# One table of steps for attention's engines: the two-unit order, doubled runs of value products and a block-diagonal left tile

## The chip, the cores and the metric

The kernel runs on one core of a Trainium2 chip. The metric is the device time of one execution in microseconds. Of the kernel before there are three runs: median 634.83 us, from 632.91 to 635.03. One further execution was recorded by the profiler; it spans 631.5 us, and all rows below are of that one. A difference of 0.5% is about what a measurement of this kernel can tell.

## The reference

Three layers follow one another: attention over 4 batches of 8 heads (576 rows of 64 values each) that keeps only scores near each row's maximum, a soft mixture of 8 experts with 4 slots each, and a gated feed-forward layer. All is float32.

```python
scores = scale * np.matmul(q, k.transpose(0, 1, 3, 2))
thresh = np.max(scores, axis=-1, keepdims=True) - tau
scores = np.where(scores >= thresh, scores, -1000000000.0)
attn = np.exp(scores - np.max(scores, axis=-1, keepdims=True))
attn = attn / (np.sum(attn, axis=-1, keepdims=True) + 1e-09)
x = np.matmul(attn, v)                     # heads side by side: 2304 x 512
...
logits = x @ phi                           # 32 slots
d = softmax(logits, axis=0);  slot_input = d.T @ x
h = np.maximum(slot_input[e] @ w1[e], 0.0);  slot_out[e] = h @ w2[e]
x = softmax(logits, axis=1) @ slot_out
...
h = x @ w_in
return (h * (1.0 / (1.0 + np.exp(-1.702 * h)))) @ w_out
```

## The kernel before

**Units and tiles.** A unit is one pair of heads of one batch: 16 units (NU), 4 to a batch. Of a head's 576 rows 512 make four tiles of 128, and the last 64 are the left rows (R). A unit has nine score tiles (TPU): four pairs, one tile for each head, and a ninth that holds the left rows of both heads. `scores` (line 392) makes a pair at once: the two heads lie on the two halves of the partitions, so their products run in the two half arrays of TensorE (form 64\*128 in the profile, rows by columns), two halves of 288 columns each, two passes for each product. The left tile's products use quarter arrays (64\*64). A score tile takes two of the eight PSUM banks, and there are two such tiles (`ps_s`).

**One tile's way.** `row_max` (416) on VectorE copies the scores to SBUF (p) and finds the row's extreme; GpSimd adds the threshold (th); `exps` (435) on ScalarE; `mask` (442) on VectorE multiplies and sums (l); `trans` (497) transposes the weights by 128\*128 products with ident on TensorE, into one of two banks (`ps_t`), and its `after` copies them on ScalarE (pt, ptr). When four or five tiles (a half) are done, `inverse`, `widen` and `across` turn the sums' reciprocals into a row (l, lw, l_row), and `attn_v` (556) multiplies with the values: v_left in the full array, then for each of four blocks kc the two heads' products in the two column halves (form 128\*64). VectorE scales the result into xt (`o_ps`, one bank).

**Other steps.** `prep_main` and `prep_rest` transpose the next unit's q and k; they, `x_rows` and the logits take the same two banks `ps_t` or parts of the bank `r_ps`. At the end of a batch the logits of 32 slots are made, their running maximum and slot sums updated. Pieces of w_in are decoded beside it, on ScalarE, VectorE and GpSimd (`decoding`, 153), one piece in five steps (PACE). Loads are issued on SP's queue.

**What sets the order.** A loop over tiles i (line 800) calls each step at a fixed distance: row_max(i-1), exps(i-1), trans(i-4), scores(i) at even tiles, mask(i-2), and, counted from a unit's start, the reciprocals at 6 and 11, the row's transposes at 9 and 14, blocks of value products at 10, 12, 14 and 16. What a step leaves behind (`after`) is called in the next round. The class InOrder (line 124) records each operation (so all of attention's operations have line 134 in the profile) and keeps it in the program's order on its engine; SP's loads are not kept so.

**Behind attention.** When attention's pools close, weights of the experts are loaded into rings a, b, c and so on, each placed in a freed pool (`swap`, line 118; the DMAs of lines 913 and 101). The expert products (L968, L1003) and the feed-forward part (L1176 to L1204) follow. The change does not touch them.

Of the kernel before, what the change touches and what calls it, by code (L numbers as in the profile page):

```python
# [8 lines left out]
F32 = mybir.dt.float32  # L9
# [10 lines left out]
def kernel(  # L20
# [37 lines left out]
    PACE = 5  # L58
# [94 lines left out]
    def decoding(pool, key, n, finish):  # L153
# [7 lines left out]
        if key[0] == "in":  # L161
            po.tensor_scalar(
                out=rest, in0=lo, scalar1=2.0 ** -52, scalar2=1.0, op0=ALU.mult, op1=ALU.mult
            )
# [72 lines left out]
    def attention():  # L237
# [28 lines left out]
        ve.memset(v_left, 0.0)  # L266
        xt = tx.tile([P, HP, C * P], F32, name="xt")
# [8 lines left out]
        def load_rests(b):  # L276
            n = {}
            for nm, src in (("q", q), ("k", k)):
                r = ldq.tile([R, H, D], F32, tag=nm + "r", name=f"{nm}r")
                nc.sync.dma_start(out=r, in_=src[b, :, C * P:S, :].rearrange("h p d -> p h d"))  # L280
                n[nm] = r
            rest[b] = n
# [32 lines left out]
        def turned(u, nm):  # L315


            if (u, nm) not in qk:
                n = S if nm == "q" else S + R
# [3 lines left out]
        def prep_rest(u, bank):  # L323
            b, hp = divmod(u, HP)
            t = bank([P, 2, R], "rem_t")
            for j, nm in enumerate("qk"):
                te.transpose(
                    t[:, j, :],
                    rest[b][nm][:, 2 * hp:2 * hp + 2, :].rearrange("p h d -> p (h d)"),
                    ident[0:R, 0:R],  # L330
                )
# [9 lines left out]
        def prep_main(u, nm, bank):  # L341
# [7 lines left out]
            def after():  # L349
                out, src = turned(u, nm)[:, R:S], t.rearrange("p c t -> p (c t)")  # L350
                if nm == "q":
                    ac.activation(out=out, in_=src, func=AF.Copy, scale=neg if u else 1.0)
                else:
                    ac.copy(out=out, in_=src)
# [37 lines left out]
        def scores(i):  # L392
# [3 lines left out]
            qx, kx = qk[u, "q"], qk[u, "k"]  # L396
            heads = [slice(h * D, (h + 1) * D) for h in range(2)]
            if t < 2 * C:
                both = [ps_s.tile([P, 2, 512], F32, tag="s", name="s_ps") for _ in range(2)]
                s_ps[i], s_ps[i + 1] = both  # L400
                c0 = R + t // 2 * P
# [14 lines left out]
        def row_max(i):  # L416

            u, t = divmod(i, TPU)
            if t % 2 == 0:
# [6 lines left out]
                scalar1=1.0 if u else neg, scalar2=None, op0=ALU.mult, op1=ALU.min,  # L426
# [3 lines left out]
            if t % 2 or t == 2 * C:  # L430
                mns.pop((u, t // 2))
            thr[i] = sm.tile([P, 1], F32, tag="th", name="th")
            po.tensor_tensor(out=thr[i], in0=mn, in1=tau_p, op=ALU.add)

        def exps(i):
            e = sx.tile([P, S], F32, tag="e", name="e_sb")
            ac.activation(
                out=e, in_=weights(i), func=AF.Exp, bias=m_neg.pop(i), scale=-1.0
# [3 lines left out]
        def mask(i):  # L442
# [3 lines left out]
            if t in (0, C):  # L446
# [6 lines left out]
            if t in (C - 1, 2 * C):  # L453
# [865 lines left out]
```

## Time and profile before

| | |
|---|---|
| median of 3 runs | 634.83 us (632.91 to 635.03) |
| the profiled execution's span | 631.5 us |
| TensorE (PE) busy | 610.9 us, 97% |
| VectorE (DVE) | 400.4 us, 63% |
| ScalarE (ACT) | 371.5 us, 59% |
| GpSimd (POOL) | 151.0 us, 24% |
| first scores | 10.7 us |
| end of attention (slot sums scaled) | 354.5 us |
| first products of the slot outputs with w_in (wq) | 395.3 us |

Records of matmuls overlap, since the engine is pipelined; so in the timeline one reads from one row's start to the next row's start. A product of two passes shows as two records: a run of four score products has x8. The span has three stages: attention to 354.5 us, the experts to 395 us, the feed-forward layer to the end. The waits are told by the instruction that waits and by what released it.

### The profile page before, as it was taken

Reading aid. Unit: us, or ns where it says so; the run is one execution under the profiler, and the core shown is the slowest. Engines: PE = TensorE matmul, PEld = TensorE weight load, DVE = VectorE, ACT = ScalarE, POOL = GpSimd, SP = SyncE. Lnnn points to the kernel's source line nnn. Section 1 sums busy time; section 2 is a strip of 40 time slices with the busy share of each in tenths; the row PEclk is TensorE's granted clock in tenths of the full one; section 3 lists DMA queues with packets and bytes.
Section 4 is the critical chain, followed back from the end, with each engine's and each line's share of the span. In section 5 each row is a group of like instructions: output and inputs, shape, how many; then the busy total and the mean of one; then the engine's idle time right before and its main releaser. Section 6 shows DMA issues by size and latency. Waiting matters only on the chain.

```text
span 631.5 us, 10661 instructions
## 1 busy us (share of the span) xinstructions
PE 610.9 (97%) x3778; PEld 417.3 (66%) x3778; DVE 400.4 (63%) x1015; ACT 371.5 (59%) x776; POOL 151.0 (24%) x309
## 2 busy tenths in 40 slices
PE   7999999999999999999998999899999999999996
PEld 5666665666666666665665642577877788888884
DVE  2987877787886877778773242999995221332422
ACT  2878877777786787877773010757576353333340
POOL 0445453354443354543341010000300000000000
PEclk9999999999999999999999989999999999999999
DMA  7984222232232132224517999333520000020203
GB/s 186 314 283 112 69 58 63 55 90 65 56 81 53 52 86 70 70 51 149 171 57 269 326 390 377 101 104 101 167 101 0 1 0 1 16 85 1 102 1 100
DMA packets 67110, 69.97 MB, mean 111 GB/s; under 512 B 42736, under 2 KB 46832, under 8 KB 67056
## 3 DMA queue, kind: packets, MB, share of 16 engines
q1 hardware_dynamic: 67056, 69.28, 34.7%
q8 instruction: 30, 0.49, 0.3%
q14 instruction: 24, 0.20, 0.1%
HBM read 64.55 MB, written 4.72 MB: 110 GB/s over the span
## 4 chain that ended last, share of the span: by engine, by line
PE 85%; DVE 5%; DMA 5%; ACT 2%; issue 1%; SPq 1%; DVEq 0%
PE s_ps L134 15%; PE o_ps L134 14%; PE pt_ps L134 11%; PE y_ps L1202 10%; PE y_ps L1203 10%; PE y_ps L1204 10%; PE r_ps L134 5%; DMA w_b<-in_moe_w_dram 3%; PE h_ps L1176 2%; DMA raw<-in_moe_w_out_dram 2%; PE acc L968 2%; PE q_t L134 2%; PE k_t L134 2%; DVE p L134 1%; PE x_ps L134 1%
## 5 line engine op out<-in xcount | busy, mean ns | idle before, releaser
L134 DVE TENSOR_SCALAR_CACHE_REDUCE p<-s_ps 128x576 f32<-128x576 f32 x135 | 101.7, 754 | 55.1 <-PE s_ps L134 49.0
L134 ACT ACTIVATE e_sb<-p,mn 128x576 f32<-128x576 f32 x144 | 111.7, 777 | 39.2 <-DVE p L134 36.1
L134 DVE SCALAR_TENSOR_TENSOR p<-p,th,e_sb 128x576 f32<-128x576 f32 x144 | 118.7, 825 | 0.7 <-ACT e_sb L134 0.7
L1202 PE MATMUL y_ps<-wo_h,gh 128*128 128x512 f32 x288 | 114.1, 397 | 0.7 <-ACT gh L1163 0.4
L1203 PE MATMUL y_ps<-wo_l,gh 128*128 128x512 f32 x288 | 113.4, 394 | 0.0
L1204 PE MATMUL y_ps<-wo_h,gw 128*128 128x512 f32 x288 | 112.7, 394 | 0.0
L134 PE MATMUL s_ps<-kx,qx 64*128 64x288 f32 (+1 forms) x640 | 104.5, 430 | 0.4 <-DVE p L134 0.4
L1165 DVE TENSOR_TENSOR gw<-sg,gh 128x768 fp32r<-128x768 f32 (+2 forms) x49 | 45.8, 938 | 88.2 <-ACT gh L1163 88.2
L134 POOL TENSOR_TENSOR th<-mn,few 128x1 f32<-128x1 f32 x144 | 58.1, 404 | 175.3 <-DVE p L134 169.8
L134 PE MATMUL pt_ps<-ident,p 128*128 128x128 f32 x580 | 91.5, 281 | 0.8 <-DVE l L134 0.6
L1181 ACT ACTIVATE sg<-h_ps 128x512 f32<-128x512 f32 (+1 forms) x96 | 42.5, 491 | 82.5 <-PE h_ps L1176 82.2
L134 PEld LDWEIGHTS pt_ps<-ident,p 128*128 128x128 f32 x580 | 63.7, 141 | 36.7 <-ACT pt L134 10.7
L134 ACT COPY pt<-pt_ps 128x512 f32<-128x512 f32 x142 | 81.6, 575 | 4.1 <-PE pt_ps L134 3.6
L134 PE MATMUL o_ps<-pt,vn 128*64 128x320 f32 (+1 forms) x512 | 75.8, 418 | 0.0
L134 PEld LDWEIGHTS s_ps<-kx,qx 64*128 64x128 f32 (+1 forms) x640 | 56.4, 177 | 24.4 <-issue 9.0
L1202 PEld LDWEIGHTS y_ps<-wo_h,gh 128*128 128x128 f32 x288 | 53.9, 187 | 14.9 <-ACT gh L1163 1.1
L1204 PEld LDWEIGHTS y_ps<-wo_h,gw 128*128 128x128 f32 x288 | 53.8, 187 | 13.2
L1203 PEld LDWEIGHTS y_ps<-wo_l,gh 128*128 128x128 f32 x288 | 53.9, 187 | 11.2 <-DVE gw L1165 0.2
L134 PEld LDWEIGHTS o_ps<-pt,vn 128*64 128x64 f32 x512 | 31.2, 136 | 30.3 <-issue 16.5
L1163 ACT CAST gh<-sg 128x768 fp32r<-128x768 f32 (+2 forms) x49 | 40.2, 823 | 1.2
L134 ACT COPY ptr<-r_ps 128x128 f32<-128x128 f32 (+1 forms) x92 | 22.8, 248 | 19.2 <-PE r_ps L134 19.0
L134 ACT ACTIVATE y<-raw 128x256 f32<-128x256 f32 (+1 forms) x44 | 23.8, 541 | 9.7 <-DMA raw<-in_moe_w_out_dram 6.9
(187 smaller groups left out, 714.1 us busy)
## 6 DMA issues: line engine op xcount, KB each, us to landing
raw<-in_moe_w_out_dram SPq DMA_DIRECT2D x16, 512.0 KB, 3.5
raw<-in_moe_w_in_dram SPq DMA_DIRECT2D x24, 256.0 KB, 2.9
w_a<-in_moe_w_dram SPq DMA_DIRECT2D x12, 512.0 KB, 6.6
w_a<-in_moe_w_dram SPq DMA_DIRECT2D x6, 1024.0 KB, 11.7
vn<-in_v_dram SPq DMA_DIRECT2D x16, 256.0 KB, 2.8
qn<-in_q_dram SPq DMA_DIRECT2D x15, 256.0 KB, 3.3
kn<-in_k_dram SPq DMA_DIRECT2D x15, 256.0 KB, 3.3
w_m<-in_moe_w_dram SPq DMA_DIRECT2D x6, 512.0 KB, 5.8
```

The lines of the kernel that those rows point to most:

```text
L134: ins = call(*args, **kw)
L968: nc.tensor.matmul(acc1[j][kc * NS:(kc + 1) * NS, :], s_in[kc // 2][:, kc % 2, e * NS:(e + 1) * NS], w_rows[1, e, kc][:, j * 512:(j + 1) * ...
L1163: nc.scalar.copy(out=gh[:, a], in_=sg[:, a])
L1165: nc.vector.tensor_sub(out=gw[:, a], in0=sg[:, a], in1=gh[:, a].bitcast(F32))
L1176: nc.tensor.matmul(ps, ws[:, f * P:(f + 1) * P], cs[:, t:t + n, :].rearrange("p t n -> p (t n)"), start=True, stop=True,)
L1181: nc.scalar.activation(out=part, in_=ps, func=AF.Gelu_apprx_sigmoid)
L1202: nc.tensor.matmul(ys[t], gh[:, tk], w_h, start=first, stop=False)
L1203: nc.tensor.matmul(ys[t], gh[:, tk], w_l, start=False, stop=False)
L1204: nc.tensor.matmul(ys[t], gw[:, tk], w_h, start=False, stop=last)
```

## The change

The loop over tiles is replaced by a table, PLAN: for each step of a unit a number for units of even index, one for odd, one for the last unit. A step's place is 9 times the unit's index plus its number; all steps of all units are sorted by it and called in that order. The numbers give an order only. Steps that were one call are split so that each has its own number (threshold, sums_added, normalised, the slot steps); `two` gives an `after` a number of its own.

The names: S0 to S3 and L are the score pairs and the left tile; RM, TH, E, MK, T and C with a tile's index are row maximum, threshold, exponential, mask, transposes and their copies; LA, INV, WD, X and LR with a half's index are the sums, reciprocal, widening, transposes and copy of the l row; A00 to A13 and LV are value products by half and block, VM their scaling; Q, K, R and CQ, CK, CR the next unit's transposes and copies; DP, DY, D1 to D3, DM and DA a piece of w_in's decoding, now two pieces a unit; IQ, IV, IR, VL and DL loads.

Beside the order: the rests of q and k are loaded into one tile of 128 partitions and turned by one transpose; the left rows of q go to a block-diagonal tile q_left, so that the left tile's scores are made in the full array; the value products of a half may come in any order; ptr has a buffer for each half.

```diff
-            n = {}
-            for nm, src in (("q", q), ("k", k)):
-                r = ldq.tile([R, H, D], F32, tag=nm + "r", name=f"{nm}r")
-                nc.sync.dma_start(out=r, in_=src[b, :, C * P:S, :].rearrange("h p d -> p h d"))
+            rest[b] = r = ldq.tile([2 * R, H, D], F32, tag="rest", name="qkr")
+            for j, src in enumerate((q, k)):
+                nc.sync.dma_start(
+                    out=r[j * R:(j + 1) * R], in_=src[b, :, C * P:S, :].rearrange("h p d -> p h d")
+                )
...
-                ac.activation(out=turned(u, "q")[:, 0:R], in_=t[:, 0, :], func=AF.Copy, scale=neg if u else 1.0)
+                for h in range(2):
+                    own = slice(h * R, (h + 1) * R)
+                    ac.copy(out=q_left[u % 2][own, own], in_=t[own, 0, :])
...
-                prods = [(s_ps[i][rows], qx[rows, 0:R], kx[rows, R:]) for rows in heads]
+                prods = [(s_ps[i], q_left[u % 2], kx[:, R:])]
...
-        steps = [(half, kc) for half in range(2) for kc in ("left", 0, 1, 2, 3)]
-        def attn_v(u, j):
+        def attn_v(u, half, kc):
+            first = (u, half) not in done
+            done[u, half] = 1 if first else done[u, half] + 1
+            last = done[u, half] == C + 1
+            io = dict(start=first, stop=last, held=True, skip_group_check=True)
...
-        for i in range(total - TPU + 20):
-            if 0 <= i - 1 < total:
-                row_max(i - 1)
...
-                    else (10, 10, 10, 12, 12, 14, 14, 14, 16, 16)
...
+        PLAN = {
+            "S0": (4.482, 2.841, 3.106), "S1": (7.019, 4.231, 8.554), "S2": (8.641, 7.391, 14.021),
+            "A00": (14.212, 15.196, 200.543), "A01": (15.623, 14.734, 218.066),
...
+            for t in range(TPU):
+                i = u * TPU + t
+                at(key(f"RM{t}"), row_max, i)
+                at(key(f"TH{t}"), threshold, i)
+                at(key(f"E{t}"), exps, i)
+                at(key(f"MK{t}"), mask, i)
+                two(key(f"T{t}"), key(f"C{t}"), ("t", i), lambda i=i: trans(i))
...
+        for _, _, do, args in sorted(todo, key=lambda x: x[:2]):
+            do(*args)
```

How it moves the instructions. A row is the line, the operation, what it writes and reads, and the output's shape. First TensorE in the middle of a unit, before (s_ps of shape 64x288 is the left tile; o_ps<-pt,vn are value products, x4 two blocks of both heads):

```order
L134 MATMUL s_ps<-kx,qx 128x288 x4
L134 MATMUL x_ps<-ident,xt 128x128 x4
L134 MATMUL pt_ps<-ident,p_1976 128x128 x4
L134 MATMUL r_ps<-ident,p_1976 128x128
L134 MATMUL r_ps<-ident,lw 128x128 x3
L134 MATMUL o_ps<-ptr,v_left 128x320
L134 MATMUL o_ps<-pt,vn 64x320 x4
L134 MATMUL pt_ps<-ident,p_2036 128x128 x4
L134 MATMUL s_ps<-kx,qx 128x288 x4
L134 MATMUL pt_ps<-ident,p_2036 128x128 x4
L134 MATMUL r_ps<-ident,p_2036 128x128
L134 MATMUL o_ps<-pt,vn 64x320 x4
```

The same engine and part of a unit now:

```order
L133 MATMUL r_ps<-ident,lw 128x128 x3
L133 MATMUL o_ps<-ptr,v_left 128x320
L133 MATMUL pt_ps<-ident,p_1994 128x128 x4
L133 MATMUL r_ps<-ident,p_1994 128x128
L133 MATMUL pt_ps<-ident,p_1994 128x128 x4
L133 MATMUL s_ps<-kx,qx 128x288 x4
L133 MATMUL o_ps<-pt,vn 64x320 x8
L133 MATMUL pt_ps<-ident,p_2037 128x128 x4
L133 MATMUL r_ps<-ident,p_2037 128x128
L133 MATMUL s_ps<-kx,q_left 128x288 x2
L133 MATMUL pt_ps<-ident,p_2114 128x128 x4
L133 MATMUL r_ps<-ident,p_2114 128x128
```

The two runs of a half's value products, with transposes and scores between, have become one run of eight right behind a score run, and the left tile's scores are two products in the full array.

ScalarE around the next unit's q and k, before (e_sb is an exponential, kx and qx the copies of K and Q):

```order
L134 ACTIVATE qx<-r_ps,few 128x64
L134 COPY kx<-r_ps 128x2x64
L134 ACTIVATE qx<-q_t,few 128x512
L134 ACTIVATE e_sb<-p_2882,mn 128x576
L134 COPY pt<-pt_ps 128x4x2x64
L134 COPY ptr<-r_ps 64x64 x2
L134 COPY kx<-k_t 128x512
L134 ACTIVATE e_sb<-p_2882,mn 128x576
```

And now, in an even unit (e_sb of p_2963 is E5):

```order
L133 COPY pt<-pt_ps 128x4x2x64
L133 COPY ptr<-r_ps 64x64 x2
L133 COPY q_left<-r_ps 64x64 x2
L133 COPY kx<-r_ps 128x2x64
L133 ACTIVATE e_sb<-p_2820,mn 128x576
L133 ACTIVATE e_sb<-p_2894,mn 128x576
L133 COPY x_sb<-x_ps 128x4x128
L133 ACTIVATE e_sb<-p_2894,mn 128x576
L133 ACTIVATE qx<-q_t,few 128x512
L133 COPY kx<-k_t 128x512
L133 ACTIVATE e_sb<-p_2963,mn 128x576
```

The copies of Q and K stand together behind three exponentials and ahead of the next one.

SP's queue near its start, before (w_a and w_m are weights of the first rings; w_c stands some 80 rows further down, behind w_b):

```order
L292 DMA kn<-in_k_dram 128x8x64
L913 DMA w_m<-in_moe_w_dram 128x2x512
L150 DMA raw<-in_moe_w_in_dram 128x512
L311 DMA v_left<-in_v_dram 64x64 x2
L913 DMA w_m<-in_moe_w_dram 128x2x512 x3
L302 DMA vn<-in_v_dram 128x2x256
L150 DMA raw<-in_moe_w_in_dram 128x512
L280 DMA qr<-in_q_dram 64x8x64
```

And now:

```order
L312 DMA v_left<-in_v_dram 64x64 x2
L149 DMA raw<-in_moe_w_in_dram 128x512
L926 DMA w_m<-in_moe_w_dram 128x2x512 x3
L303 DMA vn<-in_v_dram 128x2x256
L100 DMA w_c<-in_moe_w_dram 128x8x512
L281 DMA qkr<-in_q_dram 64x8x64
```

The load of ring c has moved from the end of the attention to its first units, ahead of the second batch's rests.

## Rows read from the trace of the kernel before

**Rows 1.** The page, part 1: engine, busy us, share of span, instructions.

```profile
PE 610.9 (97%) x3778; PEld 417.3 (66%) x3778; DVE 400.4 (63%) x1015; ACT 371.5 (59%) x776; POOL 151.0 (24%) x309
```

**Rows 2.** Chain of waits in time: start us, us, what; units 3, 5, 15.

```profile
65.06 1.49 PE s_ps L134 x7
...
104.32 1.41 PE s_ps L134 x7
...
314.07 1.41 PE s_ps L134 x7
```

**Rows 3.** TensorE's timeline: start, us, engine, line, out<-in, form, shape, count.

```profile
120.91 1.24 PE L134 MATMUL s_ps<-kx,qx 64*128 64x288 f32 x8
122.08 0.40 PE L134 MATMUL r_ps<-xt,ones 32*128 32x32 f32 x2
...
158.08 0.60 PE L134 MATMUL pt_ps<-ident,p 128*128 128x128 f32 x4
158.52 0.27 PE L134 MATMUL r_ps<-ident,p 128*128 128x128 f32 x1
...
158.95 0.70 PE L134 MATMUL o_ps<-ptr,v_left 128*128 128x320 f32 x2
159.59 1.30 PE L134 MATMUL o_ps<-pt,vn 128*64 128x320 f32 x8
160.81 0.66 PE L134 MATMUL pt_ps<-ident,p 128*128 128x128 f32 x4
161.40 1.24 PE L134 MATMUL s_ps<-kx,qx 64*128 64x288 f32 x8
162.57 0.66 PE L134 MATMUL pt_ps<-ident,p 128*128 128x128 f32 x4
...
165.08 1.19 PE L134 MATMUL s_ps<-kx,qx 64*64 64x288 f32 x8
166.20 0.66 PE L134 MATMUL pt_ps<-ident,p 128*128 128x128 f32 x4
166.69 0.27 PE L134 MATMUL r_ps<-ident,p 128*128 128x128 f32 x1
166.89 1.56 PE L134 MATMUL s_ps<-kx,qx 64*128 64x288 f32 x8
168.39 0.44 PE L134 MATMUL r_ps<-ident,lw 128*128 128x128 f32 x2
```

**Rows 4.** Stretch: us, engines' busy us, PEclk, DMA share, GB/s; then ScalarE's timeline.

```profile
160.00:180.00 20.00, 20.00 (x143) 12.76 (x141) 16.18 (x49) 16.02 (x38) 10.01 (x21) 1.00 0.27 69
...
156.09 0.58 ACT L134 COPY kx<-k_t 128x512 f32<-128x512 f32 x1
156.57 0.78 ACT L134 ACTIVATE e_sb<-p,mn 128x576 f32<-128x576 f32 x1
157.24 0.58 ACT L134 COPY pt<-pt_ps 128x512 f32<-128x512 f32 x1
```

**Rows 5.** TensorE's timeline at the end of the attention.

```profile
330.61 1.19 PE L134 MATMUL s_ps<-kx,qx 64*64 64x288 f32 x8
...
339.36 2.37 PE L134 MATMUL o_ps<-pt,vn 128*64 128x320 f32 x16
...
354.54 1.08 PE L950 MATMUL si<-stack_id,y_acc 128*128 128x32 f32 x8 [0.29 <-DVE few L134]
```

**Rows 6.** Chain of waits behind the attention; then the stretch, as in Rows 4.

```profile
356.00 10.65 PE acc L968 x96
...
367.71 16.33 DMA w_b<-in_moe_w_dram
...
384.05 10.81 DMA raw<-in_moe_w_out_dram
...
360.00:380.00 20.00, 19.34 (x160) 9.43 (x155) 8.12 (x25) 2.75 (x4) 2.02 (x1) 0.91 1.04 381
```

**Rows 7.** SP's timeline: when the load of ring c is issued.

```profile
303.19 0.38 SPq L101 DMA_DIRECT2D w_c<-in_moe_w_dram  x1
```

More of the change, by code (lines that the diff above doesn't have):

```diff
@@ L437, in exps @@
             ac.activation(
[L438 removed]
+                out=e, in_=weights(i), func=AF.Exp, bias=m_neg[i], scale=-1.0
             )
@@ L594, in attn_v, with normalised @@
-            return after
+                te.matmul(o[:, 0:n], v_left, ptr[u, half][:, 0:n], **io)
+            else:
+                for h in range(2):
+                    te.matmul(
+                        o[h * D:(h + 1) * D, 0:n], vn[:, h, kc, :], p[:, h, kc, :], **io
+                    )
+            if last:
+                pt.pop((u, half))
+                ptr.pop((u, half))
+        def normalised(u, half):
+            b, hp = divmod(u, HP)
+            o = o_ps[u]
+            row = l_row.pop((u, half))
+            ve.tensor_mul(
+                out=xt[:, hp, half * 2 * P:(half + 1) * 2 * P], in0=o[:, 0:2 * P],
+                in1=row[:, 0:2 * P],
+            )
+            if half:
+                ve.tensor_mul(
+                    out=xtr[:, hp, (b % 2) * R:(b % 2 + 1) * R], in0=o[:, 2 * P:],
+                    in1=row[:, 2 * P:],
+                )
@@ new lines, in attention, with freed @@
+        for i in range(4):
+            at(i + 0.45, warm, 2)
+        for u in range(NU):
+            unit(u)
+        def freed(names, floor, do):
+            floor[0] = max([floor[0]] + [ends[n] for n in names.split()]) + 0.0001
+            at(floor[0], do)
+        at(max(ends[f"DA{d}"] for d in range(2)) + 0.0001, swap, weights_in, "b", 4)
+        tiles = range(TPU)
+        pairs = " ".join(f"S{j}" for j in range(C)) + " L"
+        floor = [0.0]
+        freed("Q K R", floor, lambda: swap(loads, "c", 4))
@@ new lines, in attention, with late @@
+        before = {n: TPU * (NU - 2) + max(PLAN[n][0:2]) for n in pairs.split()}
+        floor[0] = max([floor[0]] + list(before.values())) + 0.0001
+        at(floor[0], swap, even_units, "d", 2)
+        freed(pairs, floor, lambda: swap(odd_units, "e", 2))
+        freed(" ".join(f"MK{t}" for t in tiles), floor, lambda: swap(exp_e, "f", 1))
+        freed(" ".join(f"T{t}" for t in tiles), floor, lambda: swap(early_p2, "g", 1))
+        def late():
+            swap(late_p2, "h", 2)
+            add_ring("lg", 0)
@@ L933, in attention @@
+        freed("INV1 X0 X1 WD1", floor, late)
+        freed("A10 A11 A12 A13 LV1 LR1 VM1", floor, lambda: swap(sums, "i", 6))
+        rows_end = TPU * (NU - 1) + max(PLAN[n][2] for n in ("SS", "SSa", "XRS", "XR"))
+        floor[0] = max(floor[0], rows_end) + 0.0005
+        at(floor[0], swap, rows, "j", 2)
+        InOrder.on = IN_ORDER
+        for _, _, do, args in sorted(todo, key=lambda x: x[:2]):
+            do(*args)
         InOrder.on = False
```

378 lines of the change are left out of this document (159 added, 219 removed), and 44 rows, old and new, of the table PLAN.

## The prediction, made before the changed kernel ran

> **What bounds the kernel now.** I read the page's busy lines first, then the chain of waits in order of time, then TensorE's timeline inside one unit, then the busy times by stretch. TensorE is busy for 97% of the span [rows 1]. In the chain of waits the first score run of unit after unit stands on TensorE: units 3 to 5 begin 39.26 us apart for two (65.06 to 104.32), 19.63 us each, and unit 15 begins at 314.07 [rows 2]. Twelve units in 249.01 us are 12 x 19.63 = 235.6 and 13.4 us more, for the three batch ends among them. In the same stretch VectorE works 16.18 us of 20, ScalarE 16.02, GpSimd 10.01, at a granted clock of 1.00, its 2.4 GHz level [rows 4]. So the attention stage, over half of the span, is paid at TensorE's pitch, and what counts is what TensorE does between its columns.
>
> That shows in TensorE's timeline, from start to start [rows 3]. Four 128*128 transposes among their like take 158.08 to 158.52, 0.44 us, so 0.11 each. After a run of another form four take 0.49 (166.20 to 166.69), and between two such runs 0.59 (160.81 to 161.40): 0.05 is lost on coming back to the full form, 0.10 on leaving it. The two passes of v_left at 320 columns take 0.64 with one leaving in it, so 0.27 a pass, and 0.243 at 288 columns. A score run is four pairs of passes, 0.97; it takes 1.17 (161.40 to 162.57), 0.20 over. A run of value products at 320 columns is four pairs, 1.08; it takes 1.22, 0.14 over. The run of left scores in quarter arrays (64*64) takes 1.12 for 0.97, 0.15 over. I read the excess as one drain of 0.10 and the first weight load of the new form, which nothing covers.
>
> **The change, part by part.**
> Fewer changes of form. With entering (0.10) and coming back (0.05), a score run alone costs 0.10 + 0.20 + 0.05 = 0.35, a value run 0.10 + 0.14 + 0.05 = 0.29, the left run 0.30. Before, a unit has four score runs, four value runs and one left run, nearly all between full-form work: 4 x 0.35 + 4 x 0.29 + 0.30 = 2.86 us. The order of the changed kernel has two score runs alone (0.70) and two blocks of a score run and a doubled value run side by side: 0.10 + 0.20 + 0.14 + 0.05 = 0.49, twice. That is 1.68. Saved: 1.18 us a unit, 18.9 us in 16 units. Counted over the whole stage, the two orders have 301 and 178 changes of form, 123 fewer at some 0.15, which agrees.
> The price of a change straight from one split form to another is the weak term. The nearest rows are a score run that is followed by 32*128 work: 120.91 to 122.08, 1.17, no more than ahead of full-form work [rows 3]. I take one drain. If it cost as much as going by the full form, 0.15 x 2 a unit, 4.8 us, would come back; if the weight load hid behind the drain, up to 0.10 x 2 a unit, 3 us, would be gained.
> A page of the Trainium skill prices the uncovered load otherwise: TensorE: Matmul & The Clock Gate, section LDWEIGHTS (loading the stationary operand), gives columns divided by 1.2 ns, 107 ns for 128 columns, where the row above shows 0.05 for the full form. By that figure a unit would lose 4.15 us to changes before and 2.49 after, and the saving would be an estimated 26.5 us in place of 18.9. The trace has the duration, so it decides.
>
> The left scores. A block-diagonal q_left (128*128) makes four passes of 288 columns, 4 x 0.243 = 0.97, the same columns as four pairs of quarter arrays: nothing beside the form, counted above. The one transpose of both rests is 0.11 for two of half the size next to a score run: nothing. ScalarE copies the rest of q in two pieces for one, some 0.2 us a unit, beside TensorE; its cover goes only if ScalarE becomes the bound. The two zero fills of q_left stand on VectorE before the first unit, beside the first loads.
>
> TensorE's waits. Work of one unit in passes: 60 transposes 6.6, scores 4.85, value products 16 pairs (8 x 0.216 + 8 x 0.27 = 3.9), v_left 0.97; 16.3 us. With 2.86 that is 19.1, so some 0.5 of the 19.63 is waiting. A part of it shows: the first score run of a unit takes 1.50 (166.89 to 168.39) for 1.17, since the l row's transposes behind it wait for GpSimd [rows 3]. The table puts these transposes (X0) behind the left scores and 4 tiles' work later than the reciprocal they need, so this wait goes. What is late next? I walked two units of the new order by hand with the durations of [rows 3, 4]. The tight places are three. (a) In an even unit the copy of K (0.48) stands on ScalarE ahead of the exponential E5 (0.67) [rows 4], and K's transposes follow the 2.2 us value run, so VectorE's mask MK5 starts some 1.8 us late; behind it queue the row scaling VM1, the reciprocal and row maximum RM6. RM6's scores land 1.8 us later, so nothing passes on. (b) Q's transposes want the buffer that the five copies of T8 free: TensorE waits 0.1 to 0.2 us. (c) The next unit's first score run needs RM8 done: 0.3 us to spare. So the walk leaves about 0.1 us a unit. The bounds are 0 and the 0.5 of now; I take 0.3, near the wait that [rows 3] shows at one place of a unit. A unit then takes 16.3 + 1.68 + 0.3 = 18.25 us, for 19.63: 1.38 x 16 = 22.1 us.
>
> Batch ends, head, tail. The 13.4 us of three batch ends are work and waits: the steps are now spread over a unit and a half. I take 1 us, from 0 to 3. The head (first scores by the first loads) and the tail from the last scores (330.61) over the value run of 339.36 to the slot sums at 354.54, 24 us [rows 5], keep their work; the tail splits the last value run and is bounded by the exponentials, -2 to +2 us; I take 0.
>
> Loads. w_c (2 MB) was issued at 303.19 [rows 7], held back by the q and k loads' pool; now it follows the first w_m loads and waits for a queue slot alone. It passes some six loads of unit 4 that are needed over 10 us later. The decoding of w_in goes from one piece in five steps to two pieces a unit, so it ends two units earlier, with 0.2 piece more a unit on VectorE and GpSimd: 0.15 us of some 2 us spare a unit.
>
> Behind attention nothing changes. There the chain is products at 356.00, the transfer of w_b at 367.71 and the raw w_out at 384.05, with the DMA engines at 1.04 of their share [rows 6]. These transfers start when the attention's pools and the first expert's products free their rings, so the stage moves as a whole.
>
> Sum: 22.1 + 1 = 23 us. The profiled execution spans 631.5; 608.5 is left. The median of the runs, 634.83, lies 3.3 above that span, so the forecast is 611.5 us.
>
> **The rivals.**
> (B) The pitch gain halves: changes straight between split forms cost double (4.8 us) and TensorE's waits stay at 0.5 a unit (3.2 us more than taken). 23 - 8 = 15 us, 620 us. For it: no row shows score and value products side by side. Against it: the 1.17 of the run ahead of 32*128 work.
> (C) VectorE and ScalarE become the bound. They work 15.9 and 15.7 us of a unit of 19.63 [rows 4]; at 17.94 that is 88%. An in-order queue at 88% that waits for two others could stretch a unit by a further 1.1 us, all but 0.3 of the gain: about 630 us, within 1%, and at 1.4 no change, 634 us.
> (D) Slower: K late. E5, and MK5, VM1 and RM6 behind it, wait for K's copy in each even unit. The load of k into its one buffer stands on SP's queue behind a raw w_in load that waits for the decoding. From 1.8 us of lateness on, each microsecond goes to TensorE, since the left scores need RM6's buffer; the gain of two units (2.8 us) is gone at 4.6. At 7 us late, eight pairs lose 8 x (7 - 4.6) = 19 us: 654 us. Against it: by the walk the k load has some 10 us.
> (E) The gain is given back at the experts: were the weights' transfers bound by bandwidth from before the end of the attention, the stage would not move with it. The share of 1.04 in [rows 6] speaks for it, the ring releases against: 10 us back, 621 us.
> That the order does not do what it says is excluded: it shows the runs.
>
> **How the numbers follow.** Forecast 0.72, 605 to 618 (all bounds of its terms: no waits and 3 us of batch ends 29 us, waits as now and a longer tail 17 us). B 0.12, E 0.06, C 0.06 (half of it within 0.5%, half faster), D 0.04. A run of this kernel can tell 0.5%, about 3.2 us, from no change. Faster: 0.72 + 0.12 + 0.06 + 0.03 = 0.93, less 0.02 for what I overlook: 0.91; within 0.5%: 0.04; slower 0.05. The range reaches from a unit without waits, 605, to B and E, 621.
>
> **What would show it.** Right: units 18.0 to 18.5 us apart; TensorE's 128*64 runs 16 records long, next to 64*128 runs, with 0.10 between; four transposes at 0.59 rare; no score run of 1.5 us; the stage from the end of attention to the last output as long as before. Wrong: score runs that start late behind VectorE's row maxima (C), idle VectorE ahead of MK5 or transposes that wait for kn (D), value runs of over 2.0 us at 256 columns (B), or a longer wait for w_b (E).

## The result, and the profile after

| | before | after |
|---|---|---|
| median of 4 runs | 634.88 us | 610.81 us (609.35 to 611.89) |
| ratio, 95% interval | | 0.9634 (0.9611 to 0.9658) |
| span of the profiled execution | 631.5 us | 609.2 us |
| first score run starts | 10.64 us | 13.29 us |
| first score run of unit 15 | 314.07 us | 290.94 us |
| first expert products (acc) | 356.00 us | 331.10 us |
| wq, the feed-forward stage begins | 395.29 us | 370.88 us |

The forecast was 611.5 us. The busy times of the page, which answer to [rows 1], say where the time went: TensorE's fell by 20.8 us, nearly the whole of the 22.3 us of span, and it is busy for the same 97% of a shorter span. Time lost to a change of form counts as busy there (20.00 of 20 us in [rows 4]), and its records fell by 2% alone. VectorE and ScalarE have about the work they had:

```profile
PE 590.1 (97%) x3698; PEld 422.1 (69%) x3698; DVE 409.1 (67%) x1017; ACT 370.5 (61%) x792; POOL 154.5 (25%) x309
```

The chain of waits in order of time (start us, us, what), which answers to [rows 2] and [rows 6]. The first three rows are the first score runs of units 2 to 4, the fourth that of unit 15:

```profile
46.00 1.17 PE s_ps L133 x8
...
63.96 1.17 PE s_ps L133 x8
...
81.98 1.17 PE s_ps L133 x8
...
290.94 1.17 PE s_ps L133 x8
...
331.10 12.35 PE acc L1026 x96
...
359.22 11.26 DMA raw<-in_moe_w_out_dram
370.88 1.20 PE wq L1183 x8
```

Units are 17.96 and 18.02 us apart, 17.99 on average, where they were 19.63. That is the sum of the prediction's work and form changes, 16.3 + 1.68 = 17.98, with nothing left for waits; the view of TensorE's waits has no row from 46 to 290 us. TensorE's timeline (start us, us, engine line operation out<-in, form, shape, count) shows it inside a unit, and answers to [rows 3]:

```profile
161.34 1.24 PE L133 MATMUL s_ps<-kx,qx 64*128 64x288 f32 x8
162.51 0.65 PE L133 MATMUL pt_ps<-ident,p 128*128 128x128 f32 x4
...
164.73 1.24 PE L133 MATMUL s_ps<-kx,qx 64*128 64x288 f32 x8
165.90 2.37 PE L133 MATMUL o_ps<-pt,vn 128*64 128x320 f32 x16
168.21 0.66 PE L133 MATMUL k_t<-ident,kn 128*128 128x128 f32 x4
...
172.42 0.60 PE L133 MATMUL pt_ps<-ident,p 128*128 128x128 f32 x4
172.85 1.14 PE L133 MATMUL s_ps<-kx,q_left 128*128 128x288 f32 x4
173.83 0.38 PE L133 MATMUL r_ps<-ident,lw 128*128 128x128 f32 x2
```

Read from start to start, the score run ahead of a value run takes 1.17 (164.73 to 165.90), exactly as the one ahead of full-form transposes (161.34 to 162.51). The value run of 320 columns takes 2.31, its 2.16 of columns and 0.15. The left scores take 0.98 between full-form neighbours (0.97 was taken), and these neighbours pay nothing.

Beside TensorE the other engines are fuller, since the same work lies in a shorter unit. The stretch (columns as in [rows 4], to which the first row answers) still shows a granted clock of 1.00. In the second stretch, the beginning of the feed-forward stage, the granted clock is 0.91, so for part of it TensorE had its lower level of 1.2 GHz. The third row is the same place before the change: 1.00, the level of 2.4 GHz. TensorE was not busier there (18.18 us of 20, for 18.70), so these rows do not say why the clock fell.

```profile
160.00:180.00 20.00, 20.00 (x149) 14.06 (x149) 18.01 (x53) 16.83 (x38) 10.64 (x22) 1.00 0.26 68
371.00:391.00 20.00, 18.70 (x82) 11.96 (x83) 18.14 (x34) 14.63 (x29) 0.00 (x0) 0.91 0.22 81
...
395.00:415.00 20.00, 18.18 (x89) 12.44 (x89) 18.82 (x35) 15.48 (x31) 0.00 (x0) 1.00 0.25 81
```

The load of ring c, issued at 303.19 before [rows 7], now goes out at 43.58 (SP's timeline), and TensorE has no wait on record near it:

```profile
43.58 0.47 SPq L100 DMA_DIRECT2D w_c<-in_moe_w_dram  x1
```

The head is where time was lost. TensorE's timeline there, two rows of the kernel before and three of the changed kernel:

```profile
9.49 1.22 PE L134 MATMUL r_ps<-ident 128*128 128x128 f32 x4 [0.56 <-ACT kx L134]
10.64 2.29 PE L134 MATMUL s_ps<-kx,qx 64*128 64x288 f32 x8
...
9.58 3.78 PE L133 MATMUL r_ps<-ident 128*128 128x128 f32 x16 [1.06 <-ACT kx L133]
13.29 1.77 PE L133 MATMUL s_ps<-kx,qx 64*128 64x288 f32 x8
15.99 1.97 PE L133 MATMUL s_ps<-kx,qx 64*128 64x288 f32 x8 [0.93 <-DVE p L133]
```

The warming products multiply ident by itself and keep nothing. All eight now stand ahead of the first score run, 3.7 us of them, where two stood before (a product shows as two records). They have the numbers 0.45 to 3.45 in the order, and the first score run of an even unit has 4.482.

So the 22.3 us of span come about in this way (before less after, from the starts above and that of unit 2, 45.48 and 46.00 on the two chains): head -2.65; units 0 and 1, 2.1; units 2 to 14, 13 x 1.64 = 21.3; three batch ends 2.3 (13.4 to 11.1); unit 15 with the tail 1.8; experts -0.5; feed-forward stage -2.1.

### The profile page after: what moved, and what is told of

Same layout as the page of the kernel before. It is cut to its first block, busy times and chain, and to the rows that moved or that the text cites. A ratio compares the mean times of both kernels' runs of the same rounds, so it can differ in the third digit from the quotient of the medians.

```text
span 609.2 us, 10564 instructions
## 1 busy us (share of the span) xinstructions
PE 590.1 (97%) x3698; PEld 422.1 (69%) x3698; DVE 409.1 (67%) x1017; ACT 370.5 (61%) x792; POOL 154.5 (25%) x309
## 4 chain that ended last, share of the span: by engine, by line
PE 82%; DVE 7%; ACT 3%; DMA 3%; issue 3%; SPq 1%; POOL 0%; DVEq 0%; ACTq 0%
PE s_ps L133 14%; PE o_ps L133 13%; PE pt_ps L133 10%; PE y_ps L1260 9%; PE y_ps L1262 9%; PE y_ps L1261 9%; PE r_ps L133 5%; DMA raw<-in_moe_w_out_dram 3%; PE h_ps L1234 2%; PE acc L1026 2%; DVE y L133 2%; DVE p L133 1%; PE k_t L133 1%; PE q_t L133 1%; PE x_ps L133 1%
## 5 line engine op out<-in xcount | busy, mean ns | idle before, releaser
L133 DVE SCALAR_TENSOR_TENSOR p<-p,th,e_sb 128x576 f32<-128x576 f32 x144 | 120.8, 854 | 14.2 <-ACT e_sb L133 9.3
L133 ACT COPY pt<-pt_ps 128x512 f32<-128x512 f32 x142 | 83.9, 597 | 25.5 <-PE pt_ps L133 24.0
L133 DVE TENSOR_SCALAR_CACHE_REDUCE p<-s_ps 128x576 f32<-128x576 f32 x120 | 87.4, 750 | 7.7 <-PE s_ps L133 7.1
L133 PE MATMUL pt_ps<-ident,p 128*128 128x128 f32 x580 | 86.7, 277 | 0.8 <-ACT qx L133 0.6
L133 PE MATMUL s_ps<-kx,qx 64*128 64x288 f32 x512 | 81.5, 431 | 1.1 <-DVE p L133 1.1
L133 POOL TENSOR_TENSOR th<-mn,few 128x1 f32<-128x1 f32 x144 | 54.2, 376 | 106.5 <-DVE p L133 95.2
L133 PE MATMUL o_ps<-pt,vn 128*64 128x320 f32 (+1 forms) x512 | 69.4, 412 | 0.3 <-ACT pt L133 0.3
L1261 PEld LDWEIGHTS y_ps<-wo_l,gh 128*128 128x128 f32 x288 | 53.9, 187 | 10.9
L133 PEld LDWEIGHTS s_ps<-kx,qx 64*128 64x128 f32 x512 | 45.2, 187 | 22.3 <-issue 9.5
L133 PEld LDWEIGHTS o_ps<-pt,vn 128*64 128x64 f32 x512 | 33.8, 136 | 30.0 <-issue 10.4
L1234 PE MATMUL h_ps<-cs,ws 128*128 128x512 f32 (+1 forms) x96 | 27.2, 354 | 0.9 <-ACT sg L1239 0.7
## 6 DMA issues: line engine op xcount, KB each, us to landing
w_a<-in_moe_w_dram SPq DMA_DIRECT2D x6, 1024.0 KB, 11.1
```

The lines of the kernel that those rows point to most:

```text
L133: ins = call(*args, **kw)
L1234: nc.tensor.matmul(ps, ws[:, f * P:(f + 1) * P], cs[:, t:t + n, :].rearrange("p t n -> p (t n)"), start=True, stop=True,)
L1261: nc.tensor.matmul(ys[t], gh[:, tk], w_l, start=False, stop=False)
```

## The experiments

All ratios are to the kernel before, measured on the same chip. The changed kernel's is 0.9634. Counts of form changes in the expectations take the split transposes of the last tile as a form of their own, so they are some 30 higher than the prediction's 301 and 178; the differences agree.

**The warming products back between the first score runs.**

```diff
-        for i in range(4):
-            at(i + 0.45, warm, 2)
+        for when in (0.45, 4.49, 4.5, 7.02):
+            at(when, warm, 2)
```

> The changed kernel, with TensorE's eight warming products put back where the kernel before had them: two ahead of the first score run, four between it and the second, two behind the second, where the changed kernel has all eight ahead of the first. Theory 1: in the profile of the changed kernel the eight take 3.7 us, from 9.58 to 13.29, while the first scores' operands are ready at about 9.5, and nothing makes this time good; the head gets 2.0 to 2.6 us shorter and all that follows moves with it: 608.2 to 608.8 us, TensorE's pitch in the later units unchanged at 18.0. Rival: the early products only fill time in which VectorE (0.93 us of waiting ahead of the second score run) or the first loads hold the head anyway, or the first score run gets slower without them (2.3 us in the kernel before, 1.8 in the changed one): less than 1 us, 610 to 611 us.

607.97 us, 0.9592 (0.9578 to 0.9606); span 606.2. TensorE's timeline:

```profile
9.90 1.22 PE L133 MATMUL r_ps<-ident 128*128 128x128 f32 x4 [1.06 <-ACT kx L133]
11.05 2.29 PE L133 MATMUL s_ps<-kx,qx 64*128 64x288 f32 x8
13.27 1.21 PE L133 MATMUL r_ps<-ident 128*128 128x128 f32 x8
14.42 1.83 PE L133 MATMUL s_ps<-kx,qx 64*128 64x288 f32 x8
```

The second score run starts 1.57 us earlier though the first one is slower, the last scores of the attention 1.3 us earlier (306.04 for 307.31); units keep their pitch. So theory 1's cause acts, but less than it said: 1.3 us of its 2.0 to 2.6 reach the end of the attention, since, as the rival had it, the first score run gets slower. Another 1.5 us lie in the feed-forward stage, 236.8 us here and 238.3 in the changed kernel's recorded execution; there the granted clock after wq is 1.00 here and 0.91 in the other, and nothing shows that the edit did that. This version is faster than both kernels.

**No warming product ahead of the first score run.**

```diff
-        for i in range(4):
-            at(i + 0.45, warm, 2)
+        for when in (4.49, 4.495, 4.5, 7.02):
+            at(when, warm, 2)
```

> The changed kernel with six of the eight warming products between the first two score runs and none ahead of the first; the other two stay behind the second. In the run with two of them ahead of the first score run, these took 1.15 us from 9.90 to 11.05 while the scores' operands were ready. Theory 1 (what stands ahead of the first score run is paid in full): the first score run starts at 9.8 to 9.9, 1.1 us earlier, 606.9 us. Rival (the two products bring TensorE to its full pace, or the head is held by the q and k loads of the second unit and by VectorE): no gain or some tenths lost, 607.8 to 608.5 us.

607.84 us, 0.9587 (0.9566 to 0.9609): the same as with two ahead. The rival holds, by the first of its two reasons:

```profile
9.17 2.88 PE L133 MATMUL s_ps<-kx,qx 64*128 64x288 f32 x8 [0.46 <-ACT kx L133]
11.99 2.93 PE L133 MATMUL r_ps<-ident 128*128 128x128 f32 x12
14.84 1.71 PE L133 MATMUL s_ps<-kx,qx 64*128 64x288 f32 x8
```

The first score run starts 1.9 us earlier than with two products ahead of it and takes 2.88 for 2.29, and the six products behind it fill the time to the second, which starts no earlier (14.84 for 14.42).

**The left scores in quarter arrays again.**

```diff
-                for h in range(2):
-                    own = slice(h * R, (h + 1) * R)
-                    ac.copy(out=q_left[u % 2][own, own], in_=t[own, 0, :])
+                ac.copy(out=q_left[u % 2][:, 0:R], in_=t[:, 0, :])
...
-                prods = [(s_ps[i], q_left[u % 2], kx[:, R:])]
+                prods = [(s_ps[i][rows], q_left[u % 2][rows, 0:R], kx[rows, R:]) for rows in heads]
```

> The changed kernel, with one part undone: the left tile's scores go in quarter arrays (64*64) again, on the same order of steps. Theory 1 (the form's own price, 0.10 us to enter, 0.15 over in the run, 0.05 to come back, paid on TensorE that waits for nothing): 16 x 0.30 = 4.8 us slower than the changed kernel, about 615.6 us; the run of left scores 1.12 us where it takes 0.97, the four transposes ahead of it 0.54 for 0.44, behind it 0.49. Rival: the freed time is taken up by waits for VectorE's row maxima in the changed kernel, so that the form's price disappears in them: under 2 us slower, under 613 us.

614.57 us, 0.969 (0.9677 to 0.9704); 3.8 us slower than the changed kernel. Units are 18.22 to 18.31 apart (batch ends aside), 0.28 more, and the rows show where:

```profile
173.89 0.60 PE L133 MATMUL pt_ps<-ident,p 128*128 128x128 f32 x4
174.42 1.19 PE L133 MATMUL s_ps<-kx,q_left 64*64 64x288 f32 x8
175.54 0.44 PE L133 MATMUL r_ps<-ident,lw 128*128 128x128 f32 x2
175.82 0.60 PE L133 MATMUL pt_ps<-ident,p 128*128 128x128 f32 x4
```

The transposes ahead take 0.53 for 0.44, the run 1.12 for 0.98, the two behind it 0.28 for 0.22: 0.29 in all, the prediction's 0.30. None of it vanishes in a wait, so TensorE sets the pitch of the changed kernel.

**A full-form product between score run and value run.**

```diff
-"LV0": (12.879, 16.706, 234.578)
+"LV0": (14.200, 15.250, 234.578)
...
-"LV1": (18.087, 19.887, 408.685)
+"LV1": (18.375, 17.650, 408.685)
```

> The changed kernel, with the left keys' value product (full form, two passes) moved in between the score run and the value run that stand side by side, in both halves of every unit but the last one, so that TensorE comes back to the full form between the two split forms; the work is the same. Theory 1 (a change straight from one split form to the other costs one drain, like any other): 0.15 us for each of 30 places, 4.5 us slower than the changed kernel, about 615.3 us. Rival B of the prediction (a direct change costs as much as two): no difference, 610.8 us. The opposite (the weight load hides behind the drain in a direct change): up to 7.5 us slower, 618 us. A value run ahead of which a full-form product stands should keep its 1.88 us at 256 columns and 2.31 at 320 in every case.

(LV0 and LV1 are entries of the table.) 621.49 us, 0.98 (0.9781 to 0.9819): 10.7 us slower than the changed kernel, more than any of the three expectations. TensorE's timeline at one of the places:

```profile
148.07 1.24 PE L133 MATMUL s_ps<-kx,qx 64*128 64x288 f32 x8
149.24 0.70 PE L133 MATMUL o_ps<-ptr,v_left 128*128 128x256 f32 x2
149.87 1.95 PE L133 MATMUL o_ps<-pt,vn 128*64 128x256 f32 x16
151.75 0.44 PE L133 MATMUL pt_ps<-ident,p 128*128 128x128 f32 x2
```

The score run keeps 1.17 and the value run 1.88. The left product takes 0.63, for 0.43 among its like: 0.20 a place, 0.40 a unit. But units grew from 17.99 to 18.85, 0.86. The other 0.46 are waits: the left product had stood among transposes and had given ScalarE time to empty their banks, and where it is gone TensorE waits there. Over two units the rest's two transposes grew from 0.22 to 0.54 from start to start, the l row's from 1.09 to 1.27, the output rows' (x_ps, whose waits end with ScalarE's copies pt) from 0.97 to 1.10. So a direct change costs no more than one change (rival B falls), and how much less than two it costs is 0.20 by the rows, not what the total says: the run changed two things.

**The runs alone, in the loop's order.** First with the left scores as before, then with the block-diagonal ones as well (all the code of the change for the rests, too):

```diff
-                    else (10, 10, 10, 12, 12, 14, 14, 14, 16, 16)
+                    else (10, 11, 11, 11, 11, 14, 15, 15, 15, 15)
```

> The kernel before, with one part of the change alone: the four value products of a half stand in one run right behind a score run (offsets 11 and 15 of the loop), with the left keys' product one offset ahead. The loop, the left scores in quarter arrays and the rest of the order stay. The order then has 73 changes of form fewer than before (of 123 that the whole change takes away, by the same count 331 to 258). Theory 1 (fewer changes of form pay by themselves, 0.15 us each): 11 us faster, about 624 us, with TensorE's waits as before. Rival (the loop's order loses it again in waits, since a doubled value run holds back the transposes behind it, and only the table gets rid of these waits): under 5 us faster, over 630 us.

642.55 us, 1.0136 (1.0119 to 1.0152).

> The kernel before, with two parts of the change and without its table: value products of a half in one run behind a score run, and the left scores by the block-diagonal 128*128 array with one transposed rest. The loop's order stays. TensorE then has 213 changes of form by the count that gives 331 for the kernel before and 208 for the changed one, so nearly all that the change takes away. Theory 1 (18 to 19 of the 24 us come from the forms, the rest from waits that the table removes): 118 x 0.15 = 17.7 us faster than before, about 617 us, and the missing 6 us are seen as TensorE's waits of 0.3 to 0.5 us a unit. Rival (the table's order is worth more than the forms, since in the loop VectorE's queue holds TensorE back as soon as TensorE gets quicker): under 10 us faster, over 625 us.

643.14 us, 1.0138 (1.0116 to 1.0161). Both are 8 to 9 us slower than before, with nearly all the form changes gone in the second. Neither theory nor rival had expected a loss. TensorE's timeline of the second behind a value run, and ScalarE's of the same time:

```profile
178.14 1.95 PE L134 MATMUL o_ps<-pt,vn 128*64 128x256 f32 x16
180.02 0.33 PE L134 MATMUL r_ps<-ident,qkr 128*128 128x128 f32 x1
180.18 0.60 PE L134 MATMUL q_t<-ident,qn 128*128 128x128 f32 x4
180.62 0.60 PE L134 MATMUL pt_ps<-ident,p 128*128 128x128 f32 x4
...
183.34 0.66 PE L134 MATMUL pt_ps<-ident,p 128*128 128x128 f32 x4 [0.80 <-ACT pt L134]
183.93 1.24 PE L134 MATMUL s_ps<-kx,qx 64*128 64x288 f32 x8
```

```profile
180.38 0.27 ACT L134 COPY ptr<-r_ps 128x128 f32<-128x128 f32 x1 [2.12 <-PE r_ps L134]
...
181.14 0.69 ACT L134 ACTIVATE qx<-q_t,few 128x512 f32<-128x512 f32 x1
181.72 0.78 ACT L134 ACTIVATE e_sb<-p,mn 128x576 f32<-128x576 f32 x1
182.39 0.42 ACT L134 ACTIVATE y<-raw 128x256 f32<-128x256 f32 x1
182.71 0.58 ACT L134 COPY pt<-pt_ps 128x512 f32<-128x512 f32 x1
```

ScalarE idles 2.12 us while TensorE is in the run, then gets rests, q, transposes and K at once. It copies the transposes of 180.62 only at 182.71, behind q, an exponential and a piece of w_in, and TensorE waits for their bank. Units are 19.9 to 20.8 us apart (by the left scores, batch ends aside), where 18.45 would be left of the 19.63 if only forms changed. This place is not all. Over two units (45.54 to 86.35) K's transposes with the wait behind them take 2.59 us, for 1.02 in the changed kernel, and the score runs 11.23 for 9.37: these wait for VectorE, which empties their tiles. In the run of 67.22 the second head's products start 0.44 late, behind a row maximum that ends at 67.60.

**The scaling of the output later on VectorE, in the same variant.**

```diff
-            if o_after:
-                o_after()
-                o_after = None
+            if o_late:
+                o_late()
+            o_late, o_after = o_after, None
```

> The kernel before with runs of value products and the block-diagonal left scores (643.1 us), and in it one thing more: VectorE's scaling of a half's output, which waits for the end of the value run, stands one step of the loop later on VectorE's queue, behind the next row maximum and mask. Theory (in the loop's order the scaling waits up to 0.9 us for the end of the 2.3 us run with the next tile's row maximum behind it, so exponentials, masks and transposes come late and TensorE waits for them): a good part of what was lost comes back, 625 to 637 us. Rival (during the long run TensorE hands out neither scores nor transposes, so VectorE and ScalarE idle and fall behind, whatever their order): no gain, 640 us and more.

645.88 us, 1.0189 (1.0166 to 1.0213). No gain, though the scaling's waits for the run's end, 10.9 us from 60 to 300 us in the variant without this edit, are gone: they aren't the cause. What is left is the rival's reading, that ScalarE and VectorE get no work during the run and too much behind it. The rows of both agree with it, but no run here takes it away within the loop, so it is argued and not shown.

**The table without the runs, and without both.** The value products of a half are parted two and two by transposes or by K or q transposes (shown: the numbers of one half; the other likewise):

```diff
-"A00": (14.212, 15.196, 200.543), "A01": (15.623, 14.734, 218.066)
+"A00": (14.212, 16.460, 200.543), "A01": (16.140, 14.734, 218.066)
...
-"A03": (15.275, 15.243, 256.954)
+"A03": (16.130, 16.465, 256.954)
```

> The changed kernel, with its table but without the runs: the four value products of each half are parted two and two, with transposes that follow anyway in between, in all units but the last. The fourth corner to the kernel before (loop, parted), its variant with the runs (loop, in runs, 642.6 and 643.1 us) and the changed kernel (table, in runs, 610.8 us). By the count that gives 208 changes of form for the changed kernel, this order has 263. Theory 1 (with the table TensorE waits for little, so each change costs its 0.15 us): 55 x 0.15 = 8.2 us slower, about 619 us, units about 0.55 us longer. Theory 2, formed on the variants of the kernel before (the table is worth the most, since the loop's order turns what TensorE saves into waits): the same 619 us, so that the table without the runs gives some 16 of the 24 us. Rival (the table pays only together with the runs, since it was laid out for their durations): 630 us and more, with TensorE waiting for VectorE or ScalarE in every unit.

619.54 us, 0.9766 (0.9747 to 0.9784), as expected. Units are 18.51 and 18.66 apart, 0.60 more; the prediction's price for two value runs more is 2 x 0.29 = 0.58.

> The changed kernel's table without both of its parts that spare changes of form: value products parted two and two as in the run before this one, left scores in quarter arrays. If the prices add up on the table, 610.8 + 8.7 (parted, measured) + 3.8 (quarters, measured) = 623.3 us, so that the table's order by itself gives 11 to 12 of the 24 us and the forms the rest, though in the loop's order the forms gave nothing. If the forms alone were what pays (the prediction's working), the time would be near the kernel before less its waits: 627 us and more.

621.86 us, 0.9803 (0.9779 to 0.9828), 1.4 us under the sum of the prices. Units are 18.71 and 18.86 apart, and no score run waits any more: over two units (44.15 to 81.72) the eight runs take 9.36 us, 1.17 each. The table brings more than the order with it (the decoding's pace, the load of ring c, a second buffer for ptr), and no run takes these apart.

**Room beside TensorE.** Four fills on VectorE, four copies on ScalarE, in units 1 to 15:

```diff
             m_neg[i] = mn
+            if u and t % 2:
+                ve.memset(spent, 0.0)
```

```diff
             e_sb[i] = e
+            if i >= TPU and i % TPU % 2:
+                ac.copy(out=spent, in_=ident)
```

> The changed kernel with four fills of a 128x128 scratch tile more on VectorE in each unit but the first (0.14 us each by the fills at the start of the trace, 0.56 us a unit), behind the row maxima of every second tile. Theory 1 (TensorE sets the pitch, VectorE has 2 us to spare in a unit of 18): under 1.5 us slower. Rival C, as the kernel without the left keys' products on TensorE bears it out (it lost only 6 of 15.5 us, so the order of the table leaves VectorE and ScalarE little room): each unit gets longer by a good part of the 0.56, 4 to 8.4 us slower in all, 615 to 619 us, with TensorE waiting for row maxima.

610.78 us, 0.9636 (0.9614 to 0.9658): nothing. From 60 to 280 us the fills are 7.6 us of work, and VectorE's busy time rose by 3.2 (197.7 to 200.9), for its masks got shorter on average (0.86 to 0.83 us each): a part of what the page counts as busy had been waiting.

> The changed kernel with four copies of a 128x128 tile more on ScalarE in each unit but the first, behind the exponentials of every second tile; the counterpart of the run with fills on VectorE, which cost nothing. By the 128x128 copies of the trace, 0.16 us each from start to start, 0.64 us a unit. Theory 1 (neither engine beside TensorE is the bound): under 1.5 us slower. Rival (ScalarE's copies free the banks that the transposes go to, and are the tightest link, as TensorE's waits in the kernel without the left products suggest): 3 to 10 us slower, with TensorE waiting for ScalarE's copies of the transposes.

611.34 us, 0.9646 (0.9631 to 0.966): within the two intervals nothing, as theory 1 had it. The attention got a little longer, though: every second unit grew by 0.2 in some batches, to 18.2, and the expert products begin at 332.52 for 331.10. The total hides it, since the feed-forward stage took 236.3 us in this execution and 238.3 in the changed kernel's. 1.4 us for some 9.6 us of added work (the expectation's 0.64 a unit): so neither engine bounds the changed kernel, though VectorE is busy for 18 of 20 us, and ScalarE seems to have less room than VectorE.

**TensorE without the left keys' value products** (their terms are left out of the attention):

```diff
         def attn_v(u, half, kc):
+            if kc == "left":
+                return
...
-            last = done[u, half] == C + 1
+            last = done[u, half] == C
```

> The changed kernel without the left keys' value products on TensorE (two passes in each half of each unit, 0.97 us a unit); these terms of the attention are left out, their transposes and copies stay. Theory 1 (TensorE alone sets the pitch of the changed kernel, VectorE and ScalarE have room left): 16 x 0.97 = 15.5 us faster than the changed kernel, about 595 us, units 17.0 us apart. Rival C of the prediction (VectorE, busy for 17.3 to 19.3 of 20 us in the changed kernel's trace, is next to its limit): the units come down by less than half of that, under 8 us, over 603 us, with TensorE waiting for VectorE ahead of its score runs and transposes.

604.7 us, 0.952 (0.9492 to 0.9547): 6 us faster, not 15.5. Units alternate between 18.02 to 18.10 and 17.36. TensorE's timeline where the left product of the second half stood:

```profile
147.59 0.66 PE L133 MATMUL pt_ps<-ident,p 128*128 128x128 f32 x4
148.51 0.33 PE L133 MATMUL r_ps<-ident,p 128*128 128x128 f32 x1 [0.27 <-DVE p L133]
```

From start to start the four transposes take 0.92 for 0.44, and 0.27 of that is on record as a wait for a mask. Theory 1 fails here, and rival C's number was the nearer one; but its reason falls with the fills, which cost nothing. It is not an engine that is full; the table's order has the mask come when TensorE used to come, and a product taken out lets TensorE arrive early. The rows add up: over two units the product's 1.94 us are gone and the other rows took 1.41 more, 0.48 of it here and 0.93 at the places that grew by the same 0.93 when the product was moved away from them (a full-form product between score run and value run, above). Why every second unit stays at 18.02 is open. Of the 5.5 us by which the attention ended earlier, wq kept 3.0 (42.3 us from acc to wq for 39.8). The chain goes through a transfer of w_c of 11.59 us there, so rival E's cause can act; but it does so with the left scores in quarter arrays and with ScalarE's copies too (11.61 us, 40.6 and 41.0 from acc to wq), where the attention was longer than the changed kernel's. That a shorter attention brings it on is not shown.

## Why the prediction was right, point by point

**The bound.** TensorE sets the pitch of the changed kernel: 0.28 us more of form in a unit cost 0.28 us of pitch, while fills on VectorE cost nothing and copies on ScalarE 1.4 us in all.

**Fewer changes of form** (1.18 us a unit, 18.9 in all). The prices hold wherever TensorE doesn't wait. Two value runs: 0.58 priced, 0.60 measured. The left run: 0.30 and 0.28. The weak term, a direct change for one drain: it was taken to spare 0.15 a place, and the rows show 0.20 with the left product between. By the figure of the Trainium skill, TensorE: Matmul & The Clock Gate, section LDWEIGHTS (loading the stationary operand), loads of 64 columns on entering and 128 on coming back, with two drains of 0.10, would make an estimated 0.36 for the left run; the measured 0.28 lies nearer to the trace's price. The prediction's 4.15 and 2.49 us by that figure are each two changes (of an estimated 0.207) more than the runs it counts, 3.73 and 2.07; its 26.5 us is their difference and stands.

**TensorE's waits** (0.5 to 0.3 us a unit). This term was mis-sized: they went to nothing, the bound of the range, as the hand walk had nearly said (0.1). 1.64 us a unit are gained for 1.38 forecast. The other corners say how. Parted and with quarter arrays the table's order takes 18.79 us a unit, 0.84 less than before, of which the direct changes and the rest of the forms may be 0.31 (1.18 less 0.87); some 0.5 are waits, all that there were.

Most of them had stood in the first score run of a unit: 1.59 and 1.49 us before (at 45.41 and 65.00), 1.17 in the table alone. The prediction saw this wait and misread its cause. It took the l row's transposes behind the run to wait for GpSimd; but GpSimd's copy (first row below) ends ahead of the run of 166.89, and it is the run itself that waits. Its second head needs the tile of the left scores, whose row maximum on VectorE (second row) ends at 167.16; that head's first product starts at 167.22.

```profile
165.48 0.80 POOL L134 COPY lw<-l 128x256 f32<-128x256 f32 x1
...
166.42 0.74 DVE L134 TENSOR_SCALAR_CACHE_REDUCE p<-s_ps 128x576 f32<-128x576 f32 x1
```

In the changed kernel this row maximum ends at 174.85 and the run starts at 175.12, so the wait is gone because the row maximum comes in time, the walk's third tight place (0.3 us to spare), and not because of the l row's new place.

**What the prediction's sum hid.** It adds forms and waits as if each could be had by itself. In the loop's order runs and left scores together lost 9 us; in the table's they gained 11 (621.86 to 610.81), and the table alone 12. The tight places that the walk went through (K's copy, Q's bank, row maxima) were the right thing to look at: had they not fitted, the forms' gain could have turned into a loss, as it did in the loop. No rival had that mechanism; B's and C's figures stopped at no change.

**Batch ends, head, tail.** 1 us taken for the batch ends, 2.3 measured; the tail 0, and with unit 15 (1.38 forecast) it gave 1.8. The head was taken at 0 and lost 2.65 us, since the prediction took the first scores to wait for the first loads alone, and did not set the score run's new number against those of the warming products. With the products put back 1.3 us of it came back by the end of the attention; the rest had been made good, for behind eight products the first score run takes 1.77 us and behind two 2.29.

**Behind attention** "nothing changes": right for the experts (0.5 us), off by 2.1 in the feed-forward stage. That stage goes with the granted clock at its start. In seven of the fourteen recorded executions the clock is 1.00 over its first 40 us, and the stage took 236.2 to 237.0 us; in the other seven, the changed kernel's among them, it is 0.52 to 0.69 over the first 5 us, and the stage took 237.3 to 238.8. Kernels with the table and without it are in both groups, so I don't count this as a loss of the change; what set the lower level off, no run shows.

So the gains that were sized too small (3.1 us of units and tail, 1.3 of batch ends) and the losses not seen (2.65, 0.5, 2.1) nearly cancelled; that the total was nearer than its terms is luck. A little more of it lies in the last step from span to median. 608.5 and 3.3 make 611.8 and not 611.5, and the 3.3 holds for the kernel before alone, whose recorded execution was quicker than its median run; the changed kernel's span of 609.2 belongs to a run of 610.98, 1.8 above it.

**Rivals.** B fell by the score run's 1.17 and the value run's 2.31. C fell by the fills and copies. D: no unit is longer than its neighbours but at batch ends. E did not act in the changed kernel (0.5 us more from acc to wq); where a weights' transfer did hold the experts, nothing shows that the attention's length was the reason.

## What to carry to other kernels

Price a change of form from the rows by start to start; here such prices held to some hundredths of a microsecond, as long as the engine that pays them waited for nothing. Before gathering an engine's work into long runs, ask what its neighbours do meanwhile and what falls on them at its end: the same runs cost 8.5 us in one order and gained 8.7 in another. When numbers in an order are laid out anew, look also at the steps whose numbers stayed.

## What had not been expected

An engine busy for 18 of 20 us in the profile took 0.66 us more a unit (four fills of 0.165 us) without any change of the time. A product that TensorE does can be worth its time to it as cover: taken out (0.97 us a unit) it gave 0.28 back, and moved away from the transposes it cost 0.46 in waits.

At the start, the same score run took 2.88 us with no warming products ahead of it, 2.29 with two, 1.77 with eight, and 1.24 in the later units (durations of the rows), with TensorE idle for 0.5 to 1.1 us ahead of the first product. The granted clock of these stretches reads 1.00 in the profile, so this slowness has to be read from durations, not from that column; its cause is not shown.
